# Down by products over all token groups, with fp16 sums, and two h blocks formed at gate and up

## The chip, the cores and the metric

The kernel runs on one core of a Trainium2 chip. The metric is the device time of one execution in microseconds (us). A time is the median of several runs, and one execution more is profiled.

## The reference

```python
s = _A_ref(layernorm(x), wqkv, wo)          # linear attention, 32 heads of 32
    # phi(t) = where(t > 0, t + 1, exp(t)) + 1e-6;  kv = sum_s phi(k) v;  z = sum_s phi(k)
    # o = phi(q) kv / (phi(q) z + 1e-6);            s = o @ wo
g = silu((silu(xn @ w_gate) * (xn @ w_up)) @ w_down)   # xn: the same layernorm of x
return x + s * g
```

x is 2048 x 1024 (tokens by features), the hidden layer of the feed-forward part 3584 wide. Everything comes and goes in bf16.

## The kernel before, in words

The program has four stages. First the layer norm, the transposes and the state of the attention (to about 117 us); then gate, up, q and the attention's output s, pair by pair (to about 540 us); then down with the final silu, the product with s and the sum with x.

**Products by seven.** A matrix product of 2 x 2 blocks is done with seven block products in place of eight (Strassen and Winograd): products 1 to 7, whose operands are blocks or sums of blocks. A product of these is called *inner* if it is itself done by seven smaller ones. Per group of 256 tokens (two column tiles of 128), a plain product in down is 28 matmuls of 128 x 512 columns, an inner one 49 of 128 x 256. An inner product is a `Joint`: four steps (a: smaller products 1 and 5; b: 6 and 2; c: 7 and 3; d: 4), with copies by ScalarE (ACT) and two adds by VectorE (DVE) between the PSUM banks x and y.

**Down before.** Tokens are split in halves p of 1024, each in two groups, so four groups g. The hidden layer h stands in DRAM (`h_scratch`) as the blocks that the seven products need: 00, 10, 11, the sum of 01 and 00 (called 5), and the sum of 01 and 11 (called 7). `Group` loads 00, 10, 7, 5, 11 of its group into slots in SBUF, and DVE forms block 6 (7 + 00) and block 4 (10 - 6) in place (`mk`). `DownSet` runs the seven products of a group, group by group; the words in `DRUN` are the order. Sums of products are kept in f32, in a PSUM bank or a 128 x 512 f32 tile (`copy`, `add`). Each finished output block goes through ACT (silu) and DVE (times s), and is added to `out` by an accumulating DMA of 128 KB (`dacc`, issued by GpSimd, POOL), onto x, which was put there before. In the last group x is added by DVE. Group 0 has one inner product (`DJ`: product 3), groups 1 to 3 have six (all but 4): 19 of 28.

**Gate and up.** `gu_pair` runs one half p with one of seven blocks n of the hidden layer, for the gate, then for the up weights: 28 pairs, 11.6 us of TensorE (PE) each. ACT evicts the gate's silu to the slots of `sg_ring`; `h_done` multiplies the up tiles onto them (128 x 1024 fp16, DVE) and stores the result to the h blocks. Blocks 5 and 7 get their first term by a store and their second, h01, by a `dacc` of 256 KB, 28 of them.

**What sets the order.** Every operation goes to a planner (`Plan`). It gives each a due time from the PE work behind it, lists them, and emits one queue per engine in order: PE, ACT, DVE, POOL and SP (plain DMAs). `BOOST` is a table of numbers that moves single operations ahead or back. An operation waits on semaphores; whatever stands behind it on its queue waits too. The helpers `pe_mm` (L231), `act` (L359), `tt` (L369, DVE), `dma` (L372, SP) and `dacc` (L376, POOL) record the operations, so most rows of the profile have one of these lines, and tiles tell the rows apart: W, X, P, H and TM are parts of SBUF, `ps` is PSUM.

Of the kernel before, what the change touches and what calls it, by code (L numbers as in the profile page):

```python
# [241 lines left out]
def build_kernel(nc, A_x, A_wqkv, A_wo, B_w_gate, B_w_up, B_w_down, out, WINDOW=10, NWARM=24, NPE=4, LEAD=16.0, CLAMP=1000.0, AHEAD=4.0):  # L242
# [12 lines left out]
    with ExitStack() as es:  # L255
# [41 lines left out]
        h_scr = nc.dram_tensor("h_scratch", [4, 5, 128, NPAIR, 256], FP16)  # L297
# [275 lines left out]

        class DownSet(Set):

            def __init__(self, ops, evac, joint, last=False, pieces=()):
                Set.__init__(self, ops, evac)
                self.joint, self.apart, self.pieces = joint, 7 in joint and not last, pieces

            def copy(self, ring, b):  # L580
                s = ring.take()
                act([bank_r[b]], [s.r], s.ap(F32), ps[b][:, :], ACT.Identity)
                return s

            def add(self, o, b, s, op=ALU.add):
                ap, r = (ps[o][:, :], bank_r[o]) if isinstance(o, int) else (o.ap(F32), o.r)
                x, y = (ps[b][:, :], s.ap(F32)) if op == ALU.add else (s.ap(F32), ps[b][:, :])
                tt([bank_r[b], s.r], [r], ap, x, y, op)

            def step(self, m):  # L590
                if m in (1, 5) or m == 4 and self.apart:
                    e = balloc(True)
                    self.grp(m, e, True)
                    self.put(m, e)
                elif m == 4 and self.pieces:
                    at = [(self.b, 0, self.pieces[0])]
                    for c0, c1 in zip(self.pieces, self.pieces[1:] + (512,)):
                        f = balloc()
                        act([bank_r[self.b]], [bank_r[f], bank_r[self.b]], ps[f][:, c0:c1], ps[self.b][:, c0:c1], ACT.Identity)
                        at.append((f, c0, c1))  # L600
                    for f, c0, c1 in at:
                        self.grp(4, f, False, c0, c1)
                        self.evac(1, 0, ps[f][:, c0:c1], bank_r[f], f, c0, c1)
                        bfree(f)
                else:
                    b = {2: "a", 6: "b", 7: "b", 4: "b", 3: "c"}[m]
                    b = getattr(self, b)
                    self.grp(m, b, False)
                    if m == 2:
                        self.out(0, 0, b)  # L610
                    elif m == 6:
                        self.s1 = self.copy(s1_ring, b)
                        if 7 in self.joint:
                            bfree(b)
                    elif m == 7:
                        self.s3 = self.copy(s5_ring, b)
                    elif m == 4:
                        self.out(1, 0, b)
                    elif m == 3:
                        self.out(0, 1, b)  # L620

            def put(self, m, e):
                J = self.joint
                if m == 1:
                    if 2 in J:
                        self.s1 = self.copy(s1_ring, e)
                        if 6 in J:
                            bfree(e)
                        else:
                            self.b = e  # L630
                    else:
                        self.a, self.b = e, balloc()
                        act([bank_r[e]], [bank_r[self.b]], ps[self.b][:, :], ps[e][:, :], ACT.Identity)
                elif m == 2:
                    self.add(e, e, self.s1)
                    self.out(0, 0, e)
                elif m == 6:
                    if 7 in J:
                        self.add(self.s1, e, self.s1)
                        bfree(e)  # L640
                    else:
                        self.add(e, e, self.s1)
                        self.b, self.s1 = e, self.copy(s1_ring, e)
                elif m == 7 and self.apart:
                    self.s3 = s5_ring.take()
                    self.add(self.s3, e, self.s1)
                    bfree(e)
                elif m == 7:
                    self.add(e, e, self.s1)
                    self.b, self.s3 = e, self.copy(s5_ring, e)  # L650
                elif m == 4:
                    self.add(e, e, self.s3)
                    self.out(1, 0, e)
                elif m == 5:
                    self.add(self.s3, e, self.s3, ALU.subtract)
                    self.evac(1, 1, self.s3.ap(F32), self.s3.r, None)
                    if 3 in J:
                        self.add(self.s1, e, self.s1, ALU.subtract)
                        bfree(e)
                    else:  # L660
                        self.add(e, e, self.s1, ALU.subtract)
                        self.c = e
                elif m == 3:
                    self.add(self.s1, e, self.s1)
                    bfree(e)
                    self.evac(0, 1, self.s1.ap(F32), self.s1.r, None)
# [670 lines left out]
        HN = {"00": 0, "5": 1, "10": 2, "7": 3, "11": 4}  # L1337
        HAT = {(0, 0): ("00", "5"), (1, 0): ("10",), (1, 1): ("11", "7")}
# [12 lines left out]
        def gu_pair(p, kind, n, stats, at):  # L1351
# [16 lines left out]
            def h_done(w, i, j):  # L1368
                if w == 0:
                    return  # L1370
                s, t = sgs.pop((p, i, j)), hst.pop((i, j))
                tt([t.r, s.r], [s.r], s.ap(FP16), t.ap(FP16), s.ap(FP16), ALU.mult, True)
                h_out[i, j] = s

                def place(nm):
                    return named("h", p, nm, n), h_scr[2 * p:2 * p + 2, HN[nm], :, 2 * n:2 * n + 2, :].rearrange(
                        "h p n t -> p h (n t)")

                def tile(s):
                    return s.ap(FP16).rearrange("p (h x) -> p h x", h=2)  # L1380
                if (i, j) != (0, 1):
                    for q, nm in enumerate(HAT[i, j]):
                        r, to = place(nm)
                        dma([s.r], [r], to, tile(s), dsem("hs%d_%d" % (s.k, q)), 256 * KB)
                for q, (nm, at) in enumerate((("5", (0, 0)), ("7", (1, 1)))):
                    if (0, 1) in h_out and at in h_out and (i, j) in ((0, 1), at):
                        r, to = place(nm)
                        t = h_out[0, 1]
                        dacc([t.r, r], [r], to, tile(t), dsem("ha%d_%d" % (t.k, q)), 256 * KB)
# [77 lines left out]
        def dblock(*at):  # L1467

            if len(at) == 1:
# [7 lines left out]
              "R10": dblock((H, 70 * KB)), "T2": dblock((P, 0)), "T3": dblock((P, 14 * KB)),  # L1477
# [21 lines left out]
        def wd_sum(o, a, b, op=ALU.subtract):  # L1499
            for h in range(2):  # L1500
# [6 lines left out]
        DJ = ((3,),) + 3 * ((1, 2, 6, 7, 5, 3),)  # L1507
        dat = [(W, q * 3584) for q in range(14)] + [(TM, 12 * KB), (X, 21 * KB), (X, 24 * KB + 512), (H, 24 * KB + 512)]
        DRUN = ("1_0 1_1 2_0 2_1 6_0 6_1 7_0 7_1 4_0 4_1 5_0 5_1 j3a j3b j3c j3d",
                "j1a j1b j1c j2a j1d j2b j2c j2d j6a j7a j6b j7b j6c j6d j7c 4_0 j7d 4_1 j5a j5b j5c j3a j5d j3b j3c j3d",  # L1510
                "j1a j1b j1c j2a j1d j2b j2c j2d j6a j7a j6b j7b j6c j6d j7c j5a j7d j5b j3a j5c j3b j5d j3c 4_0 j3d 4_1")
        OVER = (0, 2, 3, 3)
        DAT = {m: tuple(dat[3 * a:3 * a + 3]) for a, m in enumerate((1, 2, 6, 5, 3, 7))}

        PIECES = (256, 384)

        class Slots:
            def __init__(self, at, size):
                self.at, self.size = at, size
                self.free = deque(range(len(at)))  # L1520

            def take(self):
                k = self.free.popleft()
                return Slot(self.at[k][0], self.at[k][1], self.size, k)

            def give(self, s):
                self.free.append(s.k)

        hslots = Slots([(X, 0), (X, 7 * KB), (X, 14 * KB), (W, 0)], 7 * KB)
        hslots.free.pop()  # L1530
        islots = Slots([(H, 14 * KB + q * 1792) for q in range(6)], 1792)
        g_ring = Places([(W, o * KB) for o in (49, 50, 51)], 1 * KB)
        sl_ring = Places([(TM, o * KB) for o in (8, 9)], 1 * KB)
# [3 lines left out]
        def hv(s, n0=0, n1=NPAIR):  # L1537
            return (s.ap(FP16).rearrange("p (n t) -> p n t", t=256)[:, n0:n1], s.sub(n0 * 512, (n1 - n0) * 512).r)

        class Group:  # L1540

# [370 lines left out]
```

## Time and profile before

| | before |
|---|---|
| median of 3 runs (lowest, highest) | 700.5 us (699.48, 700.73) |
| profiled run | 699.15 us |
| its span | 697.1 us |
| outside the span | 2.05 us |
| PE busy | 690.8 us, 4561 matmuls |
| DVE busy | 644.8 us, 1463 instructions |
| ACT busy | 427.3 us, 860 instructions |
| POOL busy | 69.2 us, 87 instructions |
| moved by DMA | 103.70 MB, 149 GB/s on average |

Busy times are times in which at least one instruction of the engine was under way; matmuls overlap, so the time of one in a stream is read from the distance of starts. A row of the timeline is: start, length, engine, line, operation, what it writes and reads, shape, count. A row of the waits is: who waited, for whom, the sum in us, how often, the longest. A group of instructions is: busy time, mean ns of one, then the idle time before them and its releasers. PEld are the weight loads, which run beside the matmuls. The granted clock is 1.00 where TensorE was not throttled.

### The profile page before, as it was taken

Reading aid. Unit: us, or ns where it says so; the run is one execution under the profiler, and the core shown is the slowest. Engines: PE = TensorE matmul, PEld = TensorE weight load, DVE = VectorE, ACT = ScalarE, POOL = GpSimd, SP = SyncE. Lnnn points to the kernel's source line nnn. Section 1 sums busy time; section 2 is a strip of 40 time slices with the busy share of each in tenths; the row PEclk is TensorE's granted clock in tenths of the full one; section 3 lists DMA queues with packets and bytes.
Section 4 is the critical chain, followed back from the end, with each engine's and each line's share of the span. In section 5 each row is a group of like instructions: output and inputs, shape, how many; then the busy total and the mean of one; then the engine's idle time right before and its main releaser. Section 6 shows DMA issues by size and latency. Waiting matters only on the chain.

```text
span 697.1 us, 12309 instructions
## 1 busy us (share of the span) xinstructions
PE 690.8 (99%) x4561; PEld 432.8 (62%) x4561; DVE 644.8 (93%) x1463; ACT 427.3 (61%) x860; POOL 69.2 (10%) x87
## 2 busy tenths in 40 slices
PE   8999999999999999999999999999999999999998
PEld 4545445565556566666666666666665458787886
DVE  6999999878999799998999999997889999998998
ACT  4877745868988958868867577776673123122323
POOL 2211000002000011011020110000201201021110
PEclk9999999999999999999999999999999999999999
DMA  9435225018322277486580476874728666676773
GB/s 301 122 92 107 46 67 175 1 67 216 82 90 87 86 181 191 152 223 150 147 205 12 107 213 218 253 225 136 182 52 221 144 206 150 182 188 166 203 192 115
DMA packets 98268, 103.70 MB, mean 149 GB/s; under 512 B 18496, under 2 KB 91584, under 8 KB 98112
## 3 DMA queue, kind: packets, MB, share of 16 engines
q1 hardware_dynamic: 87136, 92.43, 43.3%
q0 software_dynamic: 11072, 10.49, 11.9%
q8 instruction: 36, 0.59, 0.4%
q14 instruction: 24, 0.20, 0.1%
HBM read 65.54 MB, written 37.36 MB: 148 GB/s over the span
## 4 chain that ended last, share of the span: by engine, by line
PE 95%; DVE 2%; DMA 2%; ACT 0%; issue 0%; SPq 0%
PE ps L231 95%; DMA H<-in_A_wqkv_dram 1%; DMA out_dram<-W 1%; DVE H L369 1%; DVE TM L369 0%; DVE ps L369 0%; DVE H L1073 0%; PE ps L238 0%; DVE W L369 0%; SPq L372 0%; ACT W L359 0%; ACT TM L359 0%; DVE TM L1075 0%; DVE zc L1068 0%; ACT ps L359 0%
## 5 line engine op out<-in xcount | busy, mean ns | idle before, releaser
L359 ACT ACTIVATE TM<-ps 128x512 f32<-128x512 f32 (+2 forms) x354 | 176.4, 525 | 66.5 <-PE ps L231 59.4
L231 PE MATMUL ps<-X,W 128*128 128x512 f16 (+1 forms) x894 | 190.1, 337 | 0.1
L231 PE MATMUL ps<-P,W 128*128 128x512 f16 (+1 forms) x892 | 189.3, 337 | 0.0
L369 DVE TENSOR_TENSOR ps<-ps,TM 128x256 f32<-128x256 f32 (+1 forms) x338 | 165.5, 505 | 24.6 <-PE ps L231 21.3
L359 ACT ACTIVATE H<-ps 128x512 f16<-128x512 f32 (+1 forms) x175 | 103.8, 599 | 49.6 <-PE ps L231 48.5
L231 PEld LDWEIGHTS ps<-P,W 128*128 128x128 f16 (+1 forms) x892 | 87.1, 98 | 58.0 <-ACT H L359 0.3
L231 PEld LDWEIGHTS ps<-X,W 128*128 128x128 f16 (+1 forms) x894 | 86.8, 98 | 56.9 <-DVE ps L369 0.6
L359 ACT ACTIVATE ps<-ps 128x256 f32<-128x256 f32 (+2 forms) x152 | 63.1, 415 | 76.4 <-PE ps L231 72.4
L231 PE MATMUL ps<-H,X 128*128 128x512 bf16 (+4 forms) x549 | 100.4, 331 | 0.5 <-ACT X L359 0.4
L369 DVE TENSOR_TENSOR W<-W 128x256 f16<-128x256 f16 (+6 forms) x265 | 95.3, 388 | 1.5 <-ACT W L359 0.4
L231 PE MATMUL ps<-W 128*128 128x256 f16 x538 | 96.0, 273 | 0.0
L369 DVE TENSOR_TENSOR H<-H 128x1024 f16<-128x1024 f16 (+5 forms) x150 | 87.4, 599 | 4.3 <-ACT H L359 3.0
L376 POOL DMA_DIRECT2D h_scratch<-H x28 | 33.6, 1249 | 441.8 <-DMA h_scratch<-H 120.2
L231 PEld LDWEIGHTS ps<-H,X 128*128 128x128 f16 x549 | 52.3, 98 | 37.9 <-issue 0.6
L369 DVE TENSOR_TENSOR TM<-ps,TM 128x512 f32<-128x512 f32 x99 | 67.6, 686 | 7.2 <-PE ps L231 6.6
L231 PE MATMUL ps<-H,W 128*128 128x512 f16 (+2 forms) x318 | 70.2, 347 | 0.0
L231 PEld LDWEIGHTS ps<-W 128*128 128x128 f16 (+1 forms) x538 | 52.3, 98 | 28.1 <-DVE zc L1068 0.3
L231 PE MATMUL ps<-H 128*128 128x256 f16 (+4 forms) x446 | 62.6, 273 | 0.0
L231 PE MATMUL ps<-W,H 128*128 128x256 f16 (+1 forms) x279 | 48.5, 309 | 0.3 <-ACT TM L359 0.3
L231 PEld LDWEIGHTS ps<-H 128*128 128x128 f16 (+1 forms) x446 | 39.5, 98 | 14.1
L231 PEld LDWEIGHTS ps<-H,W 128*128 128x128 f16 (+1 forms) x318 | 30.7, 98 | 28.0 <-DVE ps L369 0.3
L369 DVE TENSOR_TENSOR H<-ps,TM 128x512 f16<-128x512 f32 (+1 forms) x63 | 42.7, 684 | 1.9 <-PE ps L231 1.3
(103 smaller groups left out, 602.2 us busy)
## 6 DMA issues: line engine op xcount, KB each, us to landing
h_scratch<-H SPq DMA_DIRECT2D x70, 256.0 KB, 3.2
X<-h_scratch SPq DMA_DIRECT2D x28, 448.0 KB, 4.0
W<-in_B_w_gate_dram SPq DMA_DIRECT2D x7, 1024.0 KB, 5.3
W<-in_B_w_up_dram SPq DMA_DIRECT2D x7, 1024.0 KB, 5.8
h_scratch<-H POOLq DMA_DIRECT2D x28, 256.0 KB, 5.7
H<-in_B_w_down_dram SPq DMA_DIRECT2D x8, 896.0 KB, 6.4
W<-in_A_x_dram SPq DMA_DIRECT2D x16, 256.0 KB, 3.1
H<-in_A_wqkv_dram SPq DMA_DIRECT2D x8, 512.0 KB, 8.3
```

Of the source, the lines that this page charges most:

```text
L231: last = h.matmul(o, l, r, start=st, stop=sp, skip_group_check=True)
L359: op = PL.op("act", reads, writes, lambda h: h.activation(o, i, func, **kw), nel(o) / 1200.0 + (0.055 if src == "ps" else 0.095))
L369: return dve(reads, writes, lambda h: h.tensor_tensor(o, a, b, op), nel(o), 1.92 if fast else 0.96)
L376: return PL.op("pool", reads, writes, lambda h: h.dma_start(o, i, accum_op=ALU.add), 1.0, sem=s, nbytes=2 * nbytes)
```

## The change: what it does

1. **Down goes product by product.** `Unit(m, g)` is product m of group g. The list `UNITS` runs product 1 and 2 of groups 0 and 1, then of 2 and 3, product 6 of all four groups, product 4 of groups 0 and 1, then products 7, 5, 3 of all four groups, and product 4 of groups 2 and 3 at the end (`final_unit`, where ACT puts the sums so far in PSUM first). All products but 4 are inner: 24 of 28.
2. **fp16 sums.** ACT evacuates each product from PSUM to fp16 tiles, scaled by 1/8, two of 128 x 512 per unit, and DVE adds them as 128 x 1024 fp16 (`post`). `finish` does silu, the product with s and the accumulation for 256 tokens at once: 12 accumulating DMAs of 256 KB in place of 24 of 128 KB, and four blocks with x added by DVE.
3. **Blocks 7 and 6 are made at gate and up.** DVE adds h01 and h11 (128 x 1024 fp16, 14 of them, ten into a ring of two slots in TM, four in place); the sum is stored as block 7 and as block 6, and block 6 gets h00 by a `dacc`. Block 5 is as before. There are 28 h accumulations as before, now for blocks 5 and 6. Down loads six blocks per group; block 4 is formed as before.
4. For the last n, the tails of three blocks are copied within SBUF, not through DRAM. Loads and sums of w_down, slots and due times are placed anew, and `BOOST` has other numbers.

The diff, cut to its core:

```diff
-        HN = {"00": 0, "5": 1, "10": 2, "7": 3, "11": 4}
-        HAT = {(0, 0): ("00", "5"), (1, 0): ("10",), (1, 1): ("11", "7")}
+        HN = {"00": 0, "5": 1, "10": 2, "7": 3, "11": 4, "6": 5}
+        HAT = {(0, 0): ("00", "5"), (1, 0): ("10",), (1, 1): ("11",), "7": ("7", "6")}
+        h7_ring = Places([(TM, 8 * KB), (TM, 12 * KB)], 2 * KB)
...
+                if i + j and (0, 1) in h_out and (1, 1) in h_out and "7" not in h_out and (i, j) != (1, 0):
+                    a, b = h_out[0, 1], h_out[1, 1]
+                    if n not in (0, S_AT):
+                        t = h7_ring.take()
+                    tt([a.r, b.r], [t.r], t.ap(FP16), a.ap(FP16), b.ap(FP16), ALU.add, True)
+                    h_out["7"] = t
+                    store(t, "7")
+                for q, (nm, at, src) in enumerate((("5", (0, 0), (0, 1)), ("6", "7", (0, 0)))):
+                    if src in h_out and at in h_out and nm not in h_out:
                         r, to = place(nm)
-                        t = h_out[0, 1]
-                        dacc([t.r, r], [r], to, tile(t), dsem("ha%d_%d" % (t.k, q)), 256 * KB)
+                        z = h_out[src]
+                        dacc([z.r, r], [r], to, tile(z), dsem("ha%d_%d" % (z.k, q)), 256 * KB)
+                        h_out[nm] = True
...
-        DJ = ((3,),) + 3 * ((1, 2, 6, 7, 5, 3),)
...
+        FINAL = (2, 3)
+        UNITS = ([(m, g) for p in range(2) for m in (1, 2) for g in (2 * p, 2 * p + 1)] + [(6, g) for g in range(4)]
+                 + [(4, g) for g in range(4) if g not in FINAL] + [(m, g) for m in (7, 5, 3) for g in range(4)])
+        PLAIN = ()
+        KM = 0.125
+        PIECES = ((0, 512), (0, 256, 384, 512))
...
+        def finish(g, j, i, t):
+            s, x = gate_in(g, j, i)
+            q = g_ring.take()
+            act([t.r], [q.r], q.ap(FP16), t.ap(FP16), ACT.Silu, "sb", scale=1.0 / KM)
+            tt([q.r, s.r], [q.r], q.ap(FP16), q.ap(FP16), s.ap(FP16), ALU.mult, True)
+            to = rows_of(g, i, j)(of)
+            if x is None:
+                dacc([q.r, named("ox", g, i, j)], [named("oo", g, i, j)], to, wide(q), dsem("oa%d" % q.k), 256 * KB)
+            else:
+                tt([q.r, x.r], [x.r], x.ap(), q.ap(FP16), x.ap(), ALU.add, True)
+                dma([x.r], [], to, x.ap().rearrange("p (w c) -> p w c", w=2), dsem("oo%d" % x.k), 256 * KB)
...
+            def put(self, w, b):
+                if self.t is None:
+                    self.t = UA[self.g] if self.m == 1 else M4[self.g] if self.m == 4 else m_ring.take()
+                act([bank_r[b]], [self.t.sub(w * KB, KB).r], self.t.ap(FP16, w * KB, KB), ps[b][:, :], ACT.Identity, scale=KM)
+                bfree(b)
+                if w:
+                    self.post()
...
+                if m == 2:
+                    add(t, t, a)
+                    finish(g, 0, 0, t)
+                elif m == 6:
+                    add(a, a, t)
+                elif m == 7:
+                    add(b, a, t)
+                    if g not in FINAL:
+                        add(M4[g], b, M4[g])
+                        finish(g, 1, 0, M4[g])
...
+            st = u.steps()
+            st[0]()
+            for fn in pending:
+                fn()
+            for fn in st[1:-1]:
+                fn()
+            u.after()
+            pending = st[-1:]
```

**Where instructions move.** PE at the start of down, before: group 0's plain products (`ps<-P,X` and `ps<-H,X` are down's, an h block against a block of w_down).

```order
L231 MATMUL ps<-P,W 128x512 x4
L231 MATMUL ps<-H,X 128x512 x28
L231 MATMUL ps<-P,X 128x512 x42
L231 MATMUL ps<-H,X 128x512 x7
L231 MATMUL ps<-P,X 128x512 x14
L231 MATMUL ps<-H,X 128x512 x28
```

The same place in the changed kernel (`P,W` is the last of up, the others are down's).

```order
L231 MATMUL ps<-H,X 128x256 x7
L231 MATMUL ps<-W,H 128x256 x7
L231 MATMUL ps<-P,W 128x512 x20
L231 MATMUL ps<-W,H 128x256 x7
L231 MATMUL ps<-H,X 128x256 x21
L231 MATMUL ps<-W,X 128x256 x7
L231 MATMUL ps<-H 128x256 x7
```

Down opens with groups of seven narrow matmuls where it opened with wide ones. Over the whole program the order has 245 more matmuls of 128 x 256 and 140 fewer of 128 x 512, and otherwise the same, 4666 in all; DVE has 1457 instructions, ACT 900.

DVE in the middle of gate and up, before: a multiply of `h_done` is a `H<-H 128x1024`.

```order
L369 TENSOR_TENSOR H<-ps,TM 128x2x256 [waits s_pe]
L369 TENSOR_TENSOR W<-W 128x256
L369 TENSOR_TENSOR H<-H 128x1024 [waits s_dve]
L369 TENSOR_TENSOR H<-H 128x512 x2
L369 TENSOR_TENSOR ps<-ps,TM 128x256 [waits s_pe]
```

And in the changed kernel, with the sum for block 7:

```order
L369 TENSOR_TENSOR H<-ps,TM 128x2x256 [waits s_pe]
L369 TENSOR_TENSOR W<-W 128x2x4x128 [waits s_dve]
L369 TENSOR_TENSOR ps<-ps,TM 128x256 [waits s_pe]
L369 TENSOR_TENSOR W<-W 128x256
L369 TENSOR_TENSOR H<-H 128x1024 [waits s_dve]
L369 TENSOR_TENSOR W<-W 128x256
L369 TENSOR_TENSOR TM<-H 128x1024 [waits d_hs0_0t,s_dve]
L369 TENSOR_TENSOR ps<-ps,TM 128x256 [waits s_pe]
```

`TM<-H 128x1024` is new; it waits for the store that last read its slot (d_hs0_0t) and stands ahead of an add between PSUM banks. Ten such sums go to TM, four are of the form `H<-H`.

ACT near 320 us, evictions of the gate into slots of h (`H<-ps`, `H<-TM`), before: slot 4 is the one that waits for d_ha4, the accumulations that last read it.

```order
L359 ACTIVATE TM<-ps 128x256 [waits s_pe]
L359 ACTIVATE H<-TM 128x2x256 [waits d_hs6_1,d_hs6_0,s_dve]
L359 ACTIVATE H<-ps 128x2x256 [waits d_ha4_0,d_ha4_1]
L359 ACTIVATE ps<-ps 128x256 [waits s_act]
L359 ACTIVATE H<-ps 128x2x256 [waits d_hs7_0,s_pe]
```

And in the changed kernel:

```order
L359 ACTIVATE TM<-ps 128x512 [waits s_act]
L359 ACTIVATE H<-ps 128x2x256 [waits d_ha4_0,s_pe]
L359 ACTIVATE ps<-ps 128x256 [waits s_act,s_pe]
L359 ACTIVATE TM<-ps 128x256
L359 ACTIVATE ps<-ps 128x256 [waits s_pe]
```

Slot 4 now waits for one accumulation. That one stands later on POOL's queue, behind d_hs5_1, the store that opened block 5, and behind DVE's multiply of h01. Bank copies (`ps<-ps`) follow the eviction in ACT's queue.

More of the change, by code (lines that the diff above doesn't have):

```diff
@@ L295, in build_kernel @@
         epsc = sbt("epsc", [128, 1], F32)
-        h_scr = nc.dram_tensor("h_scratch", [4, 5, 128, NPAIR, 256], FP16)
+        h_scr = nc.dram_tensor("h_scratch", [4, 6, 128, NPAIR, 256], FP16)
         s_scr = nc.dram_tensor("s_scratch", [S, D], FP16)
@@ L572, in step @@
                     self.out(1, 0, self.b)
[L574 to L666, printed above, removed]
@@ L1512, in build_kernel @@
[L1512 to L1527, printed above, removed]
@@ new lines, in build_kernel @@
+        m_ring = Places([(TM, o * KB) for o in (0, 2, 4, 6)], 2 * KB)
+        g_ring = Places([(W, 27 * KB + 512 + o * 2 * KB) for o in range(3)], 2 * KB)
+        sl_ring = Places([(TM, 8 * KB), (TM, 12 * KB), (W, 7 * KB)], 2 * KB)
+        xo_ring = Places([(X, o * KB) for o in (21, 23, 25)] + [(W, 4 * KB)], 2 * KB)
+        HELD = [Slot(a, o * KB, 7 * KB, g) for g, (a, o) in enumerate(((X, 21), (P, 14), (P, 21), (W, 38)))]
+        FIRST = [h_ring.take() for _ in range(2)]
+        kept = []
@@ new lines, in build_kernel, with quarter @@
+        DOWN_OF = {(0, "00"): FIRST[:2], (0, "10"): HELD[:2], (1, "10"): HELD[2:]}
+        UA = [Slot(W, 19 * KB + 512 + 2 * KB * g, 2 * KB, g) for g in range(4)]
+        UB = [Slot(W, 9 * KB + 2 * KB * g, 2 * KB, g) for g in range(4)]
+        M4 = [Slot(W, 2 * KB * g, 2 * KB, g) for g in range(2)]
+        def quarter(s, k, i, n=7):
+            v = s.ap(FP16).rearrange("p (n t) -> p n t", t=256)[:, k:k + n, 128 * i:128 * i + 128]
+            return v, grains(s.a, s.off, 512, range(k, k + n), (i,))
@@ new lines, in rows_of, with wide, gate_in @@
+        def rows_of(g, i, j):
+            row = 1024 * (g // 2) + 512 * i + 256 * (g % 2)
+            return (lambda d, w=None, c0=0, c1=512: d[row:row + 256, 512 * j + c0:512 * j + c1].rearrange("(w p) c -> p w c", p=128)
+                    if w is None else d[row + 128 * w:row + 128 * w + 128, 512 * j + c0:512 * j + c1])
+        def wide(s, c=512):
+            return s.ap(FP16).rearrange("p (w c) -> p w c", w=2)
+        def gate_in(g, j, i):
+            s = sl_ring.take()
+            dma([named("s", 2 * (g // 2) + i, w, g % 2, j) for w in range(2)], [s.r], wide(s), rows_of(g, i, j)(s_scr),
+                dsem("sl%d" % s.k), 256 * KB).urgent = 20.0
+            x = None
+            if (g, j, i) in WITH_X:
+                x = xo_ring.take()
+                dma([], [x.r], x.ap().rearrange("p (w c) -> p w c", w=2), rows_of(g, i, j)(xf), dsem("xo%s%d" % (x.a.name, x.off)),
+                    256 * KB).urgent = 20.0
+            return s, x
```

344 lines of the change are left out of this document (146 added, 198 removed).

## The prediction

> **What bounds the kernel now.** I read the busy shares first, then TensorE's waits, the chain of waits, and the busy time by stage. The profile's page opens with:
>
> ```profile
> span 697.1 us, 12309 instructions
> PE 690.8 (99%) x4561; PEld 432.8 (62%) x4561; DVE 644.8 (93%) x1463; ACT 427.3 (61%) x860; POOL 69.2 (10%) x87
> PEclk9999999999999999999999999999999999999999
> ```
>
> TensorE (PE) is busy in 99% of the span at full clock, but VectorE (DVE) is at 93%, so a saving on PE counts only while DVE keeps up. All waits of PE, over the whole program:
>
> ```profile
> PE ps L231 <- POOL TM L416: 1.4, 1, 1.4
> PE ps L238 <- DVE W L815: 1.0, 1, 1.0
> PE ps L231 <- ACT X L359: 0.4, 1, 0.4
> PE ps L231 <- ACT TM L359: 0.3, 1, 0.3
> PE ps L231 <- DMA H<-in_A_wqkv_dram: 0.2, 1, 0.2
> ```
>
> They sum to 3.3 us, nearly all at the start. The chain of waits from 123 us on (start, length, what; rows between 652 and 668 left out):
>
> ```profile
> 122.92 183.96 PE ps L231 x1184
> 306.88 0.04 issue
> 306.92 345.52 PE ps L231 x2307
> ...
> 668.77 25.41 PE ps L231 x231
> 694.17 0.02 issue
> 694.20 0.29 ACT W L359
> ```
>
> Gate, up and down are one run of matmuls; what follows the last of them takes 697.1 - 694.2 = 2.9 us. So the end is PE's work plus what PE waits for, and both must be priced. By stage (stretch and its length; then busy time of PE, PEld, DVE, ACT and POOL with counts; granted clock, DMA share, GB/s):
>
> ```profile
> 123.00:200.00 77.00, 77.00 (x468) 45.62 (x469) 66.08 (x158) 63.54 (x133) 4.97 (x4) 1.00 0.36 96
> 200.00:300.00 100.00, 100.00 (x673) 60.62 (x672) 92.52 (x225) 80.03 (x168) 5.91 (x5) 1.00 0.49 138
> 300.00:400.00 100.00, 99.97 (x646) 62.71 (x645) 95.83 (x226) 70.33 (x150) 10.80 (x9) 1.00 0.57 136
> 371.00:415.00 44.00, 44.00 (x288) 27.96 (x287) 43.71 (x108) 28.45 (x62) 3.72 (x4) 1.00 0.44 116
> 540.00:580.00 40.00, 40.00 (x215) 20.93 (x214) 39.34 (x57) 8.69 (x17) 6.71 (x7) 1.00 0.66 172
> 580.00:620.00 40.00, 40.00 (x341) 33.17 (x340) 39.30 (x73) 10.27 (x23) 6.82 (x8) 1.00 0.68 169
> ```
>
> In down (from about 540) DVE has 2% left; in gate and up it has 14% left to 200 us, 4% between 300 and 400, and 0.29 us in the 44 us from 371.
>
> **Part 1: five more products by seven inner ones.** Before, group 0 has one inner product of seven and the other groups six each, 19 of 28; now all but product 4 are inner, 24. A plain product is 28 matmuls of 512 columns, an inner one 49 of 256. Prices come from starts of back-to-back matmuls in down:
>
> ```profile
> 549.52 9.23 PE L231 MATMUL ps<-P,X 128*128 128x512 f16 x42
> 558.58 1.67 PE L231 MATMUL ps<-H,X 128*128 128x512 bf16 x7
> ...
> 590.50 1.69 PE L231 MATMUL ps<-P,H 128*128 128x256 f16 x14
> 592.03 0.93 PE L231 MATMUL ps<-W,X 128*128 128x256 f16 x7
> ```
>
> 42 of 512 take 558.58 - 549.52 = 9.06 us, 0.2157 each; 14 of 256 take 1.53, 0.1093 each. Five products: 140 x 0.2157 - 245 x 0.1093 = 30.20 - 26.78 = **-3.42 us** of PE.
>
> A weight load must hide behind each of these matmuls:
>
> ```profile
> L231 PEld LDWEIGHTS ps<-P,W 128*128 128x128 f16 (+1 forms) x892 | 87.1, 98 | 58.0 <-ACT H L359 0.3
> ```
>
> 98 ns under 109 leaves 11 ns, and 580 to 620, where nearly all is 256 wide, shows PE without a gap. So the loads stay hidden. The Trainium skill, "TensorE: Matmul & The Clock Gate", section "Back-to-back issue gap", speaks against the change: in a stream of weight loads and matmuls it gives 81 ns for 128 columns and 131 ns for 512, so halving the width does not halve the time. Interpolated (an estimate from that page) 256 columns would take 98 ns, an inner product 49 x 0.098 = 4.8 us against 28 x 0.131 = 3.7, and the five would cost 5.7 us. The trace's 0.2157 and 0.1093 disagree with it, so the sum goes by the trace.
>
> **Part 2: DVE work moves from down to gate and up.** Its prices, as start to next start:
>
> ```profile
> 385.18 0.68 DVE L369 TENSOR_TENSOR H<-H 128x1024 f16<-128x1024 f16 x1
> 385.78 0.69 DVE L369 TENSOR_TENSOR H<-ps,TM 128x512 f16<-128x512 f32 x1
> 386.38 0.42 DVE L369 TENSOR_TENSOR ps<-ps,TM 128x256 f32<-128x256 f32 x1
> 386.71 0.28 DVE L369 TENSOR_TENSOR W<-H 128x256 f16<-128x256 f16 x1
> ...
> 594.13 0.62 DVE L369 TENSOR_TENSOR X<-X 128x896 f16<-128x896 f16 x1
> 594.67 0.42 DVE L369 TENSOR_TENSOR W<-W,TM 128x512 f16<-128x512 f16 x1
> 595.01 0.62 DVE L369 TENSOR_TENSOR H<-X 128x896 f16<-128x896 f16 x1
> ```
>
> 1024 fp16 0.60, 512 f32 from PSUM 0.60, 256 f32 from PSUM 0.33, 896 fp16 0.54, 512 fp16 0.34. In down the instruction orders differ by -46 of 512 f32, -32 of 512 fp16, +10 of 256 f32, +4 of 896 and +42 of 1024: -27.6 - 10.9 + 3.3 + 2.2 + 25.2 = **-7.8 us** of DVE. ACT gets 38 instructions more, most of them here, where it is a quarter busy (10.27 of 40). This relief cannot show as time by itself, since PE does not wait there; it is what lets PE's saving through.
>
> Against it stand 14 sums of 128x1024 in gate and up (block 7 was an accumulating DMA): 14 x 0.60 = **8.4 us**. From 123 to 400 the rows above leave 10.9 + 7.5 + 4.2 = 22.6 us idle, so the amount has room. Locally it has less: spread over 417 us, 1.5 sums, 0.9 us, fall into the 44 us with 0.29 idle, 0.6 us too many unless the new order takes other work out. The bounds are 0 and 0.6; I take 0.15, because the new order does put weight sums elsewhere.
>
> **Part 3: the accumulating DMAs wait for more.** A slot of h may be overwritten once its accumulation has landed. Slot 4, which the next pair's gate reuses, is accumulated late now. Landing times of POOL's h accumulations (min/median/max), and the medians of the stores, loads and output accumulations:
>
> ```profile
> L376 POOL DMA_DIRECT2D h_scratch<-H x28: 1176/1189/1707, 163.3 to 550.1; - x28
> DMA to landing us min/median/max: 4.5/5.7/8.9
> ...
> h_scratch<-H SPq DMA_DIRECT2D x70, 256.0 KB, 3.2
> X<-h_scratch SPq DMA_DIRECT2D x28, 448.0 KB, 4.0
> X<-h_scratch SPq DMA_DIRECT2D x5, 768.0 KB, 4.5
> out_dram<-W POOLq DMA_DIRECT2D x24, 128.0 KB, 4.4
> ```
>
> Around 320 us the new order has, between the matmul that the h multiply waits for and the one that ACT's next eviction into slot 4 needs, 24 matmuls of 512 and 18 of 256: 24 x 0.2157 + 18 x 0.1093 = 7.14 us. DVE spends 2 x 0.33 + 0.34 + 0.68 = 1.68 of it to the multiply's end; 5.46 us are left for a landing of 5.7. So ACT is late by 0.24 us at the median and 3.4 at the maximum. Queued behind that eviction are the bank copies that DVE and PE read. The bounds are 0 (ACT catches up, 70% busy) and 3.4; I take 0.25, nearest to the median row.
>
> **Part 4: what I cost at nothing.** The h blocks written and read once more are about 2.8 and 2.9 MB. Loads in down are issued 8 to 12 us of PE rows ahead and land in 4.0 to 4.5. If the first ones come late, one landing of about 3 us shows. Twelve output accumulations replace 24, each twice as large; what waits for them is the end of the program and ACT, when it takes one of their three slots again. The last matmuls are cut 256, 128, 128 as before, so the tail stays at 2.9 us; the wide late accumulation is issued some 20 us before the end, far above 4.4. The tail is bounded by 0 and +1.
>
> **Sum.** -3.42 + 0.15 + 0.25 = -3.0 us. The profiled run took 699.15 us, 2.05 outside its span: 697.1 - 3.0 = 694.1 span, 696.1 for the run. The median of the runs, 700.5, lies 1.35 above the profiled run; I carry it over: **697.5 us**. Bounds of the terms: 0.6 + 3.4 + 1 against 0.4 taken give at worst about 702; at best -3.4, and the unlisted gaps of about 0.5 us gone, 696.6.
>
> **Rivals.**
> 1. *VectorE becomes the bound in gate and up* (slower). All 14 sums delay PE: 8.4 - 3.4 = +5.0, 705.5 us. It decides once more than 3.4 / 0.60, about 6 of the 14, delay PE. For it: 43.71 of 44 from 371, 95.83 of 100. Against: 22.6 us idle, and no wait of PE on DVE in the table above after the start, so DVE's work has been placed with some lead. 9%.
> 2. *The accumulation into slot 4 or its neighbours lands late.* The same reuse recurs in four pairs; at 0.7 us each, 4 x 0.7 = 2.8 us, about 700.3: no change. For it: 5.46 against 5.7, and the maximum of 8.9. Against: ACT runs ahead of PE. 10%.
> 3. *Down starts before its blocks are there.* Eight blocks in eight inner products of 49 x 0.1093 = 5.4 us: 896 KB each, 171 GB/s for h alone, where the stretches from 540 show 169 to 172 for everything. One late landing, 3 us: 700.5, no change. Against: three or four loads may be under way at once. 6%.
> 4. *Weight loads show between the narrow matmuls* (slower). The 245 stand in 35 groups of seven; one load in seven exposed costs 35 x 0.098 = 3.4 us and cancels the gain, two cost 6.9: 697.5 + 6.9 = 704.4 us. It decides from one in seven. Against it: 580 to 620 is without a gap at 341 matmuls, and 14 narrow ones keep 0.1093. 2%. This is where the page's rule of part 1 would show.
> That the change does less than it says is ruled out by the counts in the order: 245 more 256s, 140 fewer 512s.
>
> **How the numbers follow.** The forecast, -2 to -4 us, has 70%; rivals 27%; 3% is for what I have not seen. A measurement here can tell 0.2%, 1.4 us. Faster: the forecast, half of rival 2 and 1% of the rest, 0.76. Slower: rivals 1 and 4, 0.11 rounded. Same: 0.13. The range: 696.2 from the best case and 0.4 us of scatter (the three runs lie 1.25 apart), to 700.8, which takes in rivals 2 and 3 and leaves out 1, 4 and the case that all bounds meet.
>
> **What would show it.** Right: PE's busy time down by about 3.4 us with 4,666 matmuls; 256-wide pitch still 0.109; DVE in 300 to 400 about 98% and PE there still 100; DVE in down clearly below 98%; PE's waits still near 3.3 us. Wrong: PE waits on DVE with x of several in 370 to 420 (rival 1); ACT's idle time before an H eviction ended by an h_scratch accumulation and PE waiting for ACT behind it (rival 2); waits on X<-h_scratch between 540 and 580 (rival 3).

## The result

| | before | changed |
|---|---|---|
| median of the runs beside each other | 699.99 us (6 runs) | 696.01 us (6 runs) |
| lowest, highest | 699.4, 700.9 | 695.37, 697.04 |
| profiled run | 699.15 us | 696.0 us |
| its span | 697.1 us | 694.1 us |

The ratio is 0.9943, with a 95% interval of 0.9931 to 0.9956: faster by 0.57%. The forecast was 697.5 us with a range from 696.2; the median lies 0.2 us below the range. The sum gave 696.1 us for the profiled run and 694.1 us for its span; they came out at 696.0 and 694.1. Timed once more, unchanged, the new kernel had 695.97 us and a ratio of 0.9942 (0.9926 to 0.9958). Over all runs of this study the kernel before has a median of 699.6 us (73 runs, 698.4 to 701.8) and the changed one 696.0 us (11 runs).

The page of the changed kernel opens with:

```profile
span 694.1 us, 12503 instructions
PE 687.6 (99%) x4647; PEld 443.4 (64%) x4666; DVE 641.3 (92%) x1455; ACT 453.1 (65%) x898; POOL 62.9 (9%) x75
PEclk9999999999999999999999999999999999999999
```

PE's busy time fell by 690.8 - 687.6 = 3.2 us. There is one weight load for each matmul, 4666 as forecast; of the matmuls' own records 19 are missing. The waits of PE, over the whole program:

```profile
PE ps L231 <- POOL TM L416: 1.4, 1, 1.4
PE ps L231 <- DMA H<-in_A_wqkv_dram: 1.1, 2, 0.6
```

Both stand in the first 10 us; none is left after that. The narrow matmuls in down keep their distance (six groups of seven from 585.67 to 590.25, of which three rows are left out here: 4.58 / 42 = 0.1090 us each):

```profile
585.67 0.93 PE L231 MATMUL ps<-W,H 128*128 128x256 f16 x7
586.43 0.93 PE L231 MATMUL ps<-P,X 128*128 128x256 f16 x7
...
590.25 0.93 PE L231 MATMUL ps<-P,H 128*128 128x256 f16 x7
```

By stage (columns as before):

```profile
300.00:400.00 100.00, 100.00 (x644) 62.31 (x643) 97.53 (x230) 70.32 (x150) 10.73 (x9) 1.00 0.63 160
371.00:415.00 44.00, 43.97 (x285) 26.98 (x282) 43.97 (x110) 27.16 (x60) 4.77 (x4) 1.00 0.50 133
540.00:580.00 40.00, 40.00 (x368) 35.62 (x366) 39.52 (x72) 15.84 (x33) 5.95 (x5) 1.00 0.86 256
580.00:620.00 40.00, 39.84 (x311) 30.49 (x312) 39.54 (x68) 14.55 (x29) 3.62 (x3) 1.00 0.63 164
660.00:694.10 34.10, 30.97 (x256) 23.84 (x255) 22.76 (x47) 17.86 (x33) 5.85 (x5) 1.00 0.74 174
```

DVE is fuller between 300 and 400 us (97.53 after 95.83) and has 0.03 us left from 371 to 415, and still no wait of PE is listed there. In down DVE is as full as before until 620 us (39.5 of 40); what it was relieved of shows after 660, where a third of the time is idle.

**Where the time went, in one table.** For each weight load of PE I take its start in the trace and subtract the time that all matmuls ahead of it need at their pitches (0.216 us for 512 columns, 0.109 for 256, 0.056 for 128 and about 0.06 for 129; the 64 matmuls with only 32 columns of weights start in fours, 3 ns apart, and four of them count 0.109 together). What is left is all that PE lost up to there. The first column is the sum of the pitches over the program; the others are this loss, in us, at five points of that sum. A point of PE's own work comes on the clock later by the loss up to there: 540 is 546 us in the kernel before.

```
kernel             PE's own work   at 50   at 123   at 300   at 540   at the end
before                 687.30       4.99     5.80     6.16     6.15      6.64
before, once more      687.30       5.74     6.56     7.02     7.07      7.15
changed                683.85       5.49     6.10     6.51     7.11      7.01
changed, once more     683.85       5.71     6.32     6.73     7.34      7.25
```

The work fell by 3.45 us. From 50 us to the end the kernel before loses 1.65 and 1.41 us in its two profiles, the changed one 1.52 and 1.54: the change brought no new stall. What differs between profiles of one kernel stands in the first 50 us.

### The profile page after: what moved, and what is told of

It is laid out like the page before. It is cut to its first block, busy times and chain, and to the rows that moved or that the text cites. A ratio compares the mean times of both kernels' runs of the same rounds, so it can differ in the third digit from the quotient of the medians.

```text
span 694.1 us, 12503 instructions
## 1 busy us (share of the span) xinstructions
PE 687.6 (99%) x4647; PEld 443.4 (64%) x4666; DVE 641.3 (92%) x1455; ACT 453.1 (65%) x898; POOL 62.9 (9%) x75
## 4 chain that ended last, share of the span: by engine, by line
PE 96%; DMA 2%; issue 1%; DVE 1%; ACT 0%; SPq 0%; POOL 0%; POOLq 0%; DVEq 0%
PE ps L231 95%; DMA H<-in_A_wqkv_dram 1%; DMA out_dram<-W 1%; DVE W L369 0%; ACT W L359 0%; PE ps L238 0%; SPq L372 0%; POOL out_dram L376 0%; DVE X L369 0%; ACT TM L359 0%; POOLq L255 0%; ACT ps L359 0%; DVEq L223 0%
## 5 line engine op out<-in xcount | busy, mean ns | idle before, releaser
L359 ACT ACTIVATE TM<-ps 128x512 f16<-128x512 f32 (+2 forms) x387 | 194.9, 528 | 73.8 <-PE ps L231 61.7
L231 PE MATMUL ps<-X,W 128*128 128x256 f16 (+1 forms) x894 | 190.2, 337 | 0.1
L359 ACT ACTIVATE ps<-ps 128x256 f32<-128x256 f32 (+1 forms) x153 | 63.2, 414 | 57.5 <-PE ps L231 54.1
L369 DVE TENSOR_TENSOR W<-W 128x256 f16<-128x256 f16 (+4 forms) x255 | 93.4, 394 | 3.2 <-ACT W L359 2.3
L231 PE MATMUL ps<-H,W 128*128 128x512 f16 (+4 forms) x370 | 75.8, 336 | 0.2
L231 PE MATMUL ps<-H 128*128 128x256 f16 (+4 forms) x512 | 71.3, 272 | 0.1
L231 PE MATMUL ps<-H,X 128*128 128x256 f16 (+3 forms) x397 | 68.3, 315 | 1.3 <-DMA H<-in_A_wqkv_dram 1.1
L369 DVE TENSOR_TENSOR TM<-ps,TM 128x512 f32<-128x512 f32 x81 | 55.2, 685 | 4.3 <-PE ps L231 3.9
L231 PE MATMUL ps<-W,H 128*128 128x256 f16 (+1 forms) x356 | 58.3, 301 | 0.0
L231 PEld LDWEIGHTS ps<-H,X 128*128 128x128 f16 x402 | 39.0, 98 | 21.7 <-issue 1.0
```

What stands on the lines that cost most here:

```text
L231: last = h.matmul(o, l, r, start=st, stop=sp, skip_group_check=True)
L359: op = PL.op("act", reads, writes, lambda h: h.activation(o, i, func, **kw), nel(o) / 1200.0 + (0.055 if src == "ps" else 0.095))
L369: return dve(reads, writes, lambda h: h.tensor_tensor(o, a, b, op), nel(o), 1.92 if fast else 0.96)
```

## The experiments

Each ran beside the kernel before, five rounds unless said. Differences to the changed kernel are taken from its 696.0 us.

**The start: both kernels once more.** No edit; the kernel before ran one round more, the changed one five.

> The kernel before, unchanged, profiled once more. Theory (the runs of one kernel differ by when the first loads of wqkv land, and after 50 us all keep the same distance from PE's own work): its first matmuls on those loads start 0.3 to 2 us later than in the first profile, and the span is longer by the same amount, 697.4 to 699 us. Rival (the runs differ by waits spread over the program): the same start and another span.

> The changed kernel, unchanged, timed and profiled once more. Theory: 695.5 to 696.5 us, ratio 0.994 to 0.995; the stretch from 50 us on takes the same time as in the first profile within 0.3 us.

Measured: 699.69 and 695.97 us, spans 697.6 and 694.1. The first matmuls on wqkv, in the profile of before and in its second one (timeline of PE):

```profile
7.63 1.04 PE L231 MATMUL ps<-H,X 128*128 128x512 bf16 x4 [0.37 <-ACT X L359]
8.85 1.02 PE L231 MATMUL ps<-H,X 128*128 128x512 bf16 x4 [0.18 <-DMA H<-in_A_wqkv_dram]
```

```profile
8.10 1.02 PE L231 MATMUL ps<-H,X 128*128 128x512 bf16 x4 [0.90 <-ACT X L359]
9.60 1.02 PE L231 MATMUL ps<-H,X 128*128 128x512 bf16 x4 [0.48 <-DMA H<-in_A_wqkv_dram]
```

The second starts 0.75 us later there, and the table has the same 0.75 us at 50 us; its span is 0.5 longer. Over the fourteen profiles of this study the loss at 50 us runs from 4.88 to 7.31 us. The first profile of before, with 4.99, is among the luckiest starts; that of the changed kernel, 5.49, is near the middle. So the two profiles that the forecast and the result are read from understate the change by about 0.5 us: 697.6 - 694.1 = 3.5 us is the fairer pair.

**Five inner products taken back at the start of down.**

```diff
-        PLAIN = ()
+        PLAIN = {(m, 0) for m in (1, 2, 6, 7, 5)}
```

The nudges in down were carried over operation by operation. Products 7 and 5 of group 0 read blocks of w_down after the inner sums have overwritten a quarter of them, so the output is not the reference's; the work is the same.

> The changed kernel with group 0's products 1, 2, 6, 7 and 5 plain again (19 inner products of 28, as before); fp16 sums, the order by products and the sums at gate and up stay. Theory (the gain is PE's arithmetic, 0.68 us for each inner product): 5 x 0.68 = 3.4 us slower than the changed kernel, about 699.4 us, ratio to the kernel before 0.999. Rival (the gain is mostly the DVE work taken out of down): it stays below 698 us, ratio under 0.997.

Measured: 706.28 us, ratio 1.0089 (1.007 to 1.0107), 10.3 us above the changed kernel: three times what PE's arithmetic says. Its profile fell on the slowest of its six runs (708.36). The table shows why:

```
kernel             PE's own work   at 50   at 123   at 300   at 540   at the end
group 0 plain          687.30       7.31     8.55     9.83    10.59     15.32
```

The work rose by 3.45 us as forecast, this profile also has the slowest start of all, and 4.7 us are lost between 540 of PE's own work and the end, nearly all near 570 us on the clock. That this comes of an order made for another kernel is my reading and was not tried. PE waits there, for 1.9 us at the longest, and the granted clock falls behind the waits (the longest wait of PE, then busy times by stretch; this file has six more lines at its head, so L237 is `pe_mm` and L375 is `tt`):

```profile
PE ps L237 <- DVE H L375: 1.9, 1, 1.9
```

```profile
565.00:570.00 5.00, 2.52 (x18) 1.59 (x16) 2.78 (x6) 2.01 (x3) 0.00 (x0) 0.89 1.08 343
570.00:575.00 5.00, 4.54 (x34) 3.42 (x33) 4.32 (x10) 1.32 (x4) 0.00 (x0) 0.77 0.58 207
```

This run could not price the five products by itself; the next one was made for that.

**Five others taken back, in the middle of down.**

```diff
-        PLAIN = ()
+        PLAIN = {(6, g) for g in range(4)} | {(2, 3)}
```

> The changed kernel with five other products plain: product 6 of all four groups and product 2 of group 3, all in the middle of down and none at its start. 19 inner products of 28. Theory (PE's arithmetic): 5 x 0.68 = 3.4 us slower than the changed kernel, 699.4 us, ratio to the kernel before 0.9995. Rival (DVE sets the pace of down, and a plain product needs about 2.8 us less of DVE): less than 1.5 us slower, under 697.5 us.

Measured: 700.09 us, ratio 1.0012 (0.9999 to 1.0024), 4.1 us above the changed kernel. That is 0.7 us above the 3.4 expected. Of the 4.1 us, 3.45 are PE's own work. Its profile fell on the slowest of its 12 runs (703.59; the others lie between 699.26 and 701.25), and there down itself loses nothing (11.38 at 540, 11.30 at the end); the loss of 4.1 us stands near 372 us, where a load of the up weights took 11.86 us to land and DVE, and then PE, came late. The other runs were not profiled; by their times most of them lack this loss. The chain, PE's longest wait, and the stretches around it:

```profile
359.10 11.86 DMA W<-in_B_w_up_dram
370.96 0.02 issue
370.98 0.76 DVE W L375 x2
...
373.27 0.35 DVE ps L375
```

```profile
PE ps L237 <- DVE ps L375: 2.1, 1, 2.1
```

```profile
372.00:375.00 3.00, 1.33 (x8) 0.85 (x9) 3.00 (x9) 0.66 (x2) 0.00 (x0) 0.91 0.00 0
375.00:378.00 3.00, 3.00 (x12) 1.54 (x11) 2.30 (x6) 1.12 (x2) 0.00 (x0) 0.52 0.00 0
```

So the gain is PE's arithmetic, to within the scatter of the runs, and the view that less DVE work would pay for most of it (under 1.5 us for the edit) is wrong: five plain products need some 14 us less of DVE (5 x 2.8, the estimate above), and the kernel is slower all the same.

**The sums at gate and up: none, half as many more, twice, three times.** The edits come behind the scheduling, so every engine's order stays and DVE alone has less or more, at the places of the 14 sums.

```diff
         PL.schedule()
+        for o, v in H7[::2]:                       # 7 more; H7 for 14 more, twice over for 28 more
+            more(o, lambda h, v=v: h.tensor_tensor(v, v, v, ALU.max), 0.6)
```

```diff
         PL.schedule()
+        for o, v in H7:                            # none: the stores take what stood in the slots
+            PL.order.remove(o)
+            for s in o.succs:
+                s.preds.discard(o)
+                s.preds |= o.preds
```

> The changed kernel with the 14 sums for block 7 left out at gate and up; the stores take what last stood in their slots, so blocks 7 and 6 and with them the output are not the reference's. 14 x 0.60 = 8.4 us less for DVE; all else in the same order. Theory (the sums fit into idle time): no change, 695.5 to 696.4 us. Rival (DVE is the bound in gate and up, the sums already cost): 2 us or more faster, under 694.5 us.

> The changed kernel with one more DVE instruction behind every second of the 14 sums at gate and up: 7 more, 0.72 us each behind the instruction that they need, 5.0 us. Theory (DVE has about 3.7 us left in gate and up after the change: 14 more cost 6.3 of their 10.0 us, 28 more 16.3 of 20.0 us): 1 to 2 us slower than the changed kernel, 697 to 698 us. Rival (each instruction costs the same share, 6.3 of 10): 3.1 us slower, 699 us. Second rival (half of the places have idle time enough): no change.

> The changed kernel, each of the 14 sums at gate and up followed by one more DVE instruction of the same shape on the same tile (maximum of it with itself); all else in the same order. 14 x 0.60 = 8.4 us more for DVE in gate and up. Theory (the sums fit into DVE's idle time there, 22.6 us before the change, some 14 after it): PE loses at most 2 us, under 698 us. Rival (DVE is already the bound there, PE pays for each sum): about +8 us, 704 us.

> As the doubled sums, with two more instructions behind each sum: 28 x 0.60 = 16.8 us more for DVE in gate and up. Theory (idle time is used up locally, 2.5 us are left between 300 and 400 us of the changed kernel): the cost grows faster than the number of sums, PE loses 3 to 9 us, 699 to 705 us. Rival (DVE is the bound already): about +17 us, 713 us. A third view, that DVE has room everywhere: under 697 us.

| DVE instructions at the 14 places | time, us | ratio (95%) | against the changed kernel |
|---|---|---|---|
| 0 | 695.63 | 0.994 (0.9925 to 0.9954) | -0.4 |
| 14 (the change) | 696.0 | 0.9943 (0.9931 to 0.9956) | 0 |
| 21 | 699.23 | 0.9989 (0.9979 to 0.9999) | +3.2 |
| 28 | 701.78 | 1.0032 (1.0021 to 1.0043) | +5.8 |
| 42 | 712.27 | 1.0177 (1.016 to 1.0193) | +16.3 |

Taking all 14 away gains nothing that can be told from zero, and the loss of PE from 50 us on is 1.66 us without them and 1.52 with them (the table below and the one above), so the sums cost PE nothing: the theory of the prediction holds, and its rival 1 does not. What was added beyond them cost more than I had expected. For 14 more that was 2 us at most, and 5.8 came, nearer to the rival's 8. For 28 more it was 3 to 9, and 16.3 came, close to the rival's 17, that DVE is the bound already; but the first 14 sums, which cost nothing, speak against that rival. The first seven more already cost 3.2 us, where I had expected 1 to 2 from a reserve of 3.7 us that 14 and 28 more had suggested; the rival that each costs the same share gave 3.1. No common reserve shows: the first seven cost 0.46 us each (3.2 / 7). My reading is that the planner put the 14 sums where what stands behind them on DVE's queue could wait, and that one more instruction there delays the bank add behind it. The waits of PE between 123 and 545 us, with seven more and with 14 more:

```profile
PE ps L231 <- DVE ps L369: 1.1, 3, 0.6
```

```profile
PE ps L231 <- DVE ps L369: 1.9, 6, 0.5
PE ps L231 <- DVE H L369: 0.5, 1, 0.5
PE ps L231 <- DVE W L369: 0.2, 1, 0.2
```

In most of these rows it is an add between PSUM banks that comes late. They name less than the loss: a matmul's record is 379 ns long at a distance of 216 ns, so the first 0.16 us of each delay do not show as a wait. The loss spreads over the stage:

```
kernel             PE's own work   at 50   at 123   at 300   at 540   at the end
no sums                683.85       6.20     6.81     7.28     7.96      7.86
7 more                 683.85       5.16     5.77     7.00     9.67      9.93
14 more                683.85       5.39     6.00     8.05    12.51     13.33
28 more                683.85       4.88     5.48    11.16    20.72     23.00
```

**The relief in down taken back.** Behind each of the first 13 sums of products in down, one more DVE instruction of the same shape.

```diff
         PL.schedule()
+        for o, v in POST[:13]:
+            more(o, lambda h, v=v: h.tensor_tensor(v, v, v, ALU.max), 0.6)
```

> The changed kernel with one more DVE instruction of 128x1024 fp16 behind each of the first 13 sums of products in down: 13 x 0.60 = 7.8 us of DVE put back, as much as the change took out of down. Theory of the prediction (that relief lets PE's saving through): DVE is 99% busy from 540 to 620 us in the changed kernel too, so PE loses 3 to 7 us, 699 to 703 us. Rival (DVE's work there can slip to the end of down, where it is idle for a third of the time): under 697 us.

Measured: 703.67 us, ratio 1.0061 (1.0043 to 1.0078), 7.7 us above the changed kernel. That is above the 3 to 7 expected: PE pays for nearly all of the 7.8 us put back, and the rival that DVE's work can slip to the end falls. The loss rises from 6.96 at 540 to 14.49 at the end. The waits of PE from 530 us to the end:

```profile
PE ps L231 <- DVE H L369: 2.7, 2, 1.6
PE ps L231 <- DVE ps L369: 2.4, 4, 1.5
PE ps L231 <- ACT TM L359: 0.8, 1, 0.8
```

With the DVE work of before, down would have lost twice what the inner products gain. This shows the need for the relief, as far as more work at these 13 places can show it.

**The inner products alone, in the old order.** The kernel before, with its nudges in down left out in both (they belong to operations that are no longer the same); the control, and then:

```diff
-        DJ = ((3,),) + 3 * ((1, 2, 6, 7, 5, 3),)
+        DJ = 4 * ((1, 2, 6, 7, 5, 3),)
-        RUN = [DRUN[0]] + [DRUN[1]] * 2 + [DRUN[2]]
+        RUN = [DRUN[1]] * 3 + [DRUN[2]]
```

In the second kernel some operands in down are overwritten before they are read, so its output is not the reference's; number and shapes of the operations are those of 24 inner products.

> The kernel before, with the table of nudges applied up to the start of down only. A control for the next run. Theory: the nudges in down are worth a few us, 700 to 707 us.

> The control, with group 0's products inner as in the other groups (24 of 28), in the old order, group by group, with f32 sums: one part of the change alone. Theory (the order by products is what makes the five possible, since a set of w_down sums is then needed only when its product comes): six sets of sums, 4 us of DVE each, are needed in group 0's 38 us, where DVE has 2% left, so 10 to 20 us slower than the control. Rival (the inner products alone give the gain): 3.4 us faster than the control.

Measured: the control 713.79 us (ratio 1.0198), so the nudges in down are worth 14 us; 700 to 707 us was expected. All inner: 739.98 us (1.0572), 26.2 us slower than the control, more than the 10 to 20 expected. The waits of PE between 520 and 600 us in the second, and its matmuls there:

```profile
PE ps L231 <- DVE H L369: 22.2, 4, 11.0
PE ps L231 <- DVE ps L369: 2.3, 3, 0.9
PE ps L231 <- ACT ps L359: 0.5, 1, 0.5
```

```profile
549.53 1.68 PE L231 MATMUL ps<-H,X 128*128 128x256 bf16 x7 [4.88 <-DVE H L369]
562.18 3.60 PE L231 MATMUL ps<-P,W 128*128 128x512 f16 x8 [10.98 <-DVE H L369]
```

At the start of down PE waits for DVE's sums, 22 us in four waits, though its own work is the same as in the changed kernel (683.85). So without nudges the five products are not to be had in the old order; whether nudges made for it would bring them in was not tried. That the order by products lets them in, because one set of w_down sums is then due every few units, fits these waits and is not shown by itself. Which of the new order, the fp16 sums and the h sums is worth how much apart from the others was not tried.

**The accumulations issued later.** Twenty short POOL instructions ahead of each of the 28 accumulations into h blocks, 0.15 us from one to the next, so about 3 us.

```diff
+        for o in HA:      # each waits for what the accumulation waited for, and the accumulation for the last
+            for _ in range(20):
+                ... h.memset(neg_half[:], -0.5) ...
```

> The changed kernel with 20 short POOL instructions ahead of each of the 28 accumulations into h blocks, so that each is issued about 3 to 4 us later. Theory (ACT runs ahead of PE enough to take up a late slot): PE loses under 1 us, below 697 us. Rival (the landing into slot 4 stands on PE's path, as the prediction's rival 2 has it, in four pairs): 4 x 2 to 3 us slower, 704 us or more.

Measured: 699.89 us, ratio 1.0005 (0.9993 to 1.0018), 3.9 us above the changed kernel, between the two views. Its runs spread from 698.25 to 702.39 us, twice as wide as those of the changed kernel; the profile fell on the lowest. There ACT waits for the slots, and PE for ACT:

```profile
ACT H L359 <- DMA h_scratch<-H: 5.0, 3, 3.2
```

```profile
PE ps L231 <- ACT ps L359: 1.4, 1, 1.4
PE ps L231 <- ACT TM L359: 0.9, 1, 0.9
```

1.6 of the loss stands between 300 and 350 us (6.13 to 7.77), the place that the prediction's part 3 names, and 1.25 between 500 and 540. In the changed kernel itself ACT waits there too, at 325 us, once, 0.6 us, and no wait of PE is listed:

```profile
  ACT H L359: 0.6, 1
...
DMA to landing us min/median/max: 4.4/5.2/8.9
```

A landing about 3 us later costs PE a wait of 1.4 us there, so by this one place the slack between ACT's wait and PE's is about 1.6 us (an estimate): rival 2 names a real path, which was not the one that decided. DVE's instructions are as long as in the changed kernel (683 ns for a 128x1024 sum in both), so the added POOL work did not slow them.

## Why the prediction was right or wrong

- **Part 1, -3.42 us: right.** The pitches of the trace give 687.30 - 683.85 = 3.45, the narrow matmuls keep 0.1090, the waits after 50 us are the same within 0.2, and the taken-back products in the middle of down cost 4.1 with 3.45 of arithmetic; the other 0.7 is within the spread of those runs and has no cause shown. By an estimate from the figures for 128 and 512 columns in the Trainium skill, "TensorE: Matmul & The Clock Gate", section "Back-to-back issue gap", the five products would have cost 5.7 us; the measured pitches decide against it for this kernel. Rival 4 is gone with it.
- **Part 2, the relief and the sums: right in kind.** The 14 sums cost nothing that can be told from zero (0.4 us), and the relief is needed (7.7 us without). The relief was 7.2 us of DVE's busy time from 540 us on (147.96 to 140.80), near the 7.8; the sums were put too high, since without them DVE is busy 6.6 us less (641.3 to 634.7), not 8.4. Wrong was the picture behind it, of idle time that takes up what comes: 21 instructions at those places cost 3.2 us although 2.5 us stood idle between 300 and 400 in the changed kernel. As far as these runs tell, the sums were free because of where they stand, and not because DVE had time to spare: seven more right behind them took nearly all of the gain, about as rival 1 had it for six sums that delay PE. Also wrong is "DVE in down clearly below 98%": it is 99% to 620 us, and idle only from 660.
- **The 0.4 us of new stalls: wrong.** Neither the 0.15 for DVE nor the 0.25 for the slot came: the loss from 50 us to the end is 1.52 and 1.54 against 1.65 and 1.41. For the slot I had taken a late arrival at ACT for a late arrival at PE; 1.6 us lie between them.
- **The step from the profile to the median: the one that failed.** "The median of the runs, 700.5, lies 1.35 above the profiled run; I carry it over". The 1.35 was no property of the kernel. The three runs shown had a median 0.9 us above that of 73, and the profile a start 0.75 us earlier than the second one's. Measured, the step is 699.6 - 699.15 = 0.45 us for that profile, 0.0 for the second one (699.57), and 0.0 for the changed kernel (696.0). The forecast's 697.5 is 1.5 above 696.0; 0.9 of it is the three runs' median, 0.4 the stalls that did not come, and 0.2 is left, within the scatter. That the span and the profiled run came out to a tenth is partly luck: a start 0.5 us later than in the profile before (5.49 against 4.99) stands where the sum had 0.4 us of stalls.
- **The range: too narrow below.** Its lower end allowed 0.4 us of scatter for the median, when three runs alone lay 1.25 apart.
- **Rival 3** did not happen: no wait of PE on a load of h in either profile of the changed kernel. The tail holds: 694.1 less the last matmul's end at about 691.1 is 3.0 us after 2.9.

## What to carry to other kernels

Where PE runs without gaps, the difference of two kernels is the difference of their matmuls at the measured pitches, and the work is in showing that nothing new makes it wait; a table of the start of each weight load less the sum of pitches ahead of it tells both apart. Idle time of an engine whose queue runs in order should not be counted as a common reserve: here 14 instructions of about 0.6 us cost nothing where they had been placed, and seven more right behind them cost 0.46 us each. A median of three runs and one profile can each sit most of a microsecond from the kernel's middle, and where the change is 3 us that belongs in the range.

## What the runs showed of the hardware

A wait of PE can cost about twice its length, because the granted clock may fall behind it. In the run with product 6 plain, one wait of 2.1 us near 373 us was followed by 3 us at a granted clock of 0.52, and the loss was 4.1 us in all; behind waits of 4.9 and 11.0 us, in the run with all inner products in the old order, it stayed at half for some 18 us:

```profile
544.00:550.00 6.00, 1.12 (x6) 0.45 (x5) 5.93 (x8) 0.00 (x0) 0.00 (x0) 0.95 0.08 22
550.00:556.00 6.00, 1.20 (x6) 0.53 (x4) 6.00 (x9) 0.00 (x0) 0.00 (x0) 0.50 0.00 0
556.00:562.00 6.00, 0.00 (x0) 0.00 (x0) 5.90 (x9) 0.60 (x1) 0.31 (x1) 0.50 0.26 87
562.00:568.00 6.00, 4.41 (x12) 1.61 (x13) 4.95 (x8) 1.19 (x2) 1.48 (x2) 0.50 0.83 199
568.00:574.00 6.00, 5.01 (x27) 3.03 (x25) 4.77 (x8) 0.66 (x2) 1.82 (x2) 0.55 0.98 172
```

There 22.2 + 2.3 + 0.5 = 25.0 us of waits became a loss of 47.70 - 14.93 = 32.8 us between 500 and 540 of PE's own work. The Trainium skill, "TensorE: Matmul & The Clock Gate", section "What's actually happening", puts the fall to half speed behind an idle window of about 3.4 us; here a wait of 2.1 us was enough. The length of the wait alone does not decide: in the control without nudges one of 3.0 us, near 550 us, left the granted clock at 1.00 for the next 8 us (its wait and its stretches below), and so did those of up to 1.6 us in the run with the relief taken back and up to 1.4 us in the run with 28 more sums.

```profile
550.53 1.90 PE L231 MATMUL ps<-P,W 128*128 128x512 f16 x8 [3.05 <-DVE H L369]
```

```profile
547.00:551.00 4.00, 0.95 (x6) 0.24 (x4) 3.96 (x7) 0.00 (x0) 0.88 (x1) 1.00 0.89 133
551.00:555.00 4.00, 4.00 (x20) 1.83 (x19) 3.29 (x6) 1.79 (x3) 1.20 (x1) 1.00 0.94 269
555.00:559.00 4.00, 1.96 (x10) 0.69 (x7) 4.00 (x6) 0.00 (x0) 2.11 (x2) 1.00 1.05 186
```
